# One exponential tile in 32 on VectorE: four attention layers on one Trainium2 core

## The chip, the cores and the metric

The kernel runs on one core of a Trainium2 chip. The metric is the device time of one execution in microseconds. Five engines work side by side, each through its own queue of instructions: TensorE (matmuls; PE in the profile, with its weight loads as PEld), VectorE (DVE), ScalarE (ACT), GpSimd (POOL) and SyncE (SP), which here issues the DMA transfers.

## The reference

`x` is 2048 tokens by 512. Four attention layers with a residual follow one another: windowed (A), full (B), windowed, full. Each has 32 heads of 16 dimensions. All is float32.

```python
def layer(x, wqkv, wo, window):                 # A: window 256 and causal; B: no mask
    qkv = (layernorm(x) @ wqkv).reshape(B, S, 3, H, Dh)
    q, k, v = ...
    scores = jnp.einsum("bhqd,bhkd->bhqk", q, k) * (Dh ** -0.5)
    p = softmax(scores, axis=-1)                # A: masked scores at -1e9
    return x + (p @ v -> B, S, D) @ wo
x = layer(layer(layer(layer(x, A), B), A), B)
```

## The kernel before, in words

**Attention in a full layer.** Keys lie on the partitions. A query chunk `c` (four of 512 queries) and a quad `qd` (eight of four heads) are worked through key tile by key tile: `NT` = 16 tiles `j` of 128 keys. For each tile, `exps` (L705) is called for two pairs of heads. Each call makes the scores of two heads, 128 keys by 2 x 512 queries, in PSUM (L714, two matmuls of 64 contracted rows each, which occupy the array's two row halves) and one exponential of 128x1024 on ScalarE (L718) into an SBUF tile `e`. Queries and keys are split in fp16 parts, and a shift that keeps the exponential in range stands in one of the 64 rows, so the exponential needs only its scale. Score tiles rotate over three PSUM buffers in a full layer (two of the pool `s` and `PH["third"]`), `e` tiles over six.

The values are the second matmul, `pv` in `attn_full` (L750, the matmul at L758): for each of the four heads, 17 weight columns (16 dimensions and a column of ones, which sums the denominators) against the head's half of an `e` tile, in fp32, accumulated over the 16 key tiles. Each head has its own 32 columns of the array and its own 32 partitions of one PSUM bank, `acc[0]`. The profile has two matmul records for each such fp32 matmul.

**Order on TensorE.** It is written out by hand. `attention` puts each tile's `pv` in a queue, `pvq`; `flush(2)` issues the one that is two tiles old. So the values of tile `j` come behind the scores of tile `j + 2`. Behind the last `pv` of a quad stands `epilogue` (L677): VectorE transposes `acc[0]` into SBUF (L686), divides by the denominators and writes the fp16 parts of the output `o`.

**Side work.** Between the steps, `Side.step` puts in matmuls of other stages: projections of queries, keys and values for this or the next layer, and output projections. In a full layer these run as four matmuls of 32 columns each (L429), here called a side group, all into one PSUM bank, `acc[1]`, which VectorE then empties (L527 and L528 for queries and keys, L638 for values, L652 and L673 for the output). `share` decides how many groups a step gets, from a budget and a planned clock (`clock`, `spent`), in which a step takes at least 1.8 us; `PH["free"]` keeps the bank unused for 1.6 or 2.2 us of planned time after each accumulation. `Side.one` picks the first ready piece of work. Layer 1 goes through all eight quads of one query chunk and then to the next chunk; layer 3 goes through two quads (a pair, `t`) for all four chunks and then to the next pair. Layer 1's side work includes the first projections of windowed layer 2.

**Other engines.** On the engines other than TensorE the order of instructions comes from the program order and from priorities; `tc.high_priority(HEAD_START)` moves an instruction ahead in it. In the full layers ScalarE has the exponentials alone, and VectorE the evictions, the epilogues, residual additions, statistics and normalisations.

Of the kernel before, what the change touches and what calls it, by code (L numbers as in the profile page):

```python
# [32 lines left out]
HEAD_START = 100  # L33
EB, XB, XNB, WB, VB, OB = 6, 4, 4, 2, 3, 5
L_MIN = 2.0 ** -90
L_SUM = 2.0 ** 60
# [150 lines left out]
def fast_path(ctx, tc, flag, a_x, a_wqkv, a_wo, b_wqkv, b_wo, out):  # L187
# [19 lines left out]

    XC, XN, V, O, OT, KM, PH = {}, {}, {}, {}, {}, {}, {"free": 0.0}
    CM, DN, DC, WT, ST, pend = {}, {}, {}, {}, {}, []

    clock, DONE, XNR, ONR = [0.0], {}, {}, {}
# [286 lines left out]
    def project(l, s, c, act, ht=None, first=None):  # L498
# [14 lines left out]
        for t in range(NHT) if ht is None else (ht,):  # L513
# [8 lines left out]
            e = first[2][:, t:t + 1] if first else es[:, ty, s, t:t + 1]  # L522
            with tc.high_priority(HEAD_START):
                if act:
                    nc.scalar.activation(sp[:, 0], ps, AF.Copy, scale=e)  # L525
                else:
                    nc.vector.tensor_scalar(sp[:, 0], ps, e, None, op0=ALU.mult)  # L527
                nc.vector.scalar_tensor_tensor(sp[:, 1], ps, e, sp[:, 0], op0=ALU.mult, op1=ALU.subtract)  # L528
# [28 lines left out]
    def keys(l, c, act, ht=None, first=None):  # L557
        sqs = yield from project(l, 1, c, act, ht, first)

        def rest():  # L560
            ph = squares(f"k{l}_{c}_{ht}", sqs)
            if l not in KM:
                KM[l] = vp.tile([P, NQ], F32, name=f"km{l}", tag="km", bufs=2)
            r = quarters(ht)
            with tc.high_priority(HEAD_START):
                nc.vector.tensor_reduce(KM[l][r, c:c + 1], ph[r], axis=AX.X, op=ALU.max)  # L566
        pend.append((clock[0] + 3.6, rest))
# [73 lines left out]
    def wo(l, c, tail):  # L641
# [4 lines left out]
        for i in range(4):  # L646
# [3 lines left out]
            k = 4 * c + i  # L650
            with tc.high_priority(HEAD_START):
                nc.vector.tensor_tensor(d, ps, gcol[l % 2], ALU.mult)  # L652
# [25 lines left out]
    def epilogue(l, c, qd, a):  # L678
# [5 lines left out]
        ot = vp.tile([P, QC // 32, 32], F32, name=f"ot{n}", tag="oe")  # L684
        with tc.high_priority(HEAD_START if l % 2 else 0):
            nc.vector.transpose(ot.rearrange("p b r -> p (b r)"), a)  # L686
# [19 lines left out]
    def exps(name, kt, qt, pr, pieces):  # L706

        turn["s"] += 1
        ps = PH["third"] if PH["full"] and turn["s"] % 3 == 0 else ps_s.tile([P, 2, QC], F32, name=f"s{name}", tag="s")
        w0 = min(p[3] for p in pieces)  # L710
        w1 = max(p[3] + p[2] for p in pieces)
        for kc, qc, wd_, s0 in pieces:
# [3 lines left out]
        spent(0.27)  # L716
        e = pp.tile([P, 2, QC], F32, name=f"e{name}", tag="e", bufs=EB)
        nc.scalar.activation(e[:, :, w0:w1], ps[:, :, w0:w1], AF.Exp, scale=SCALE)  # L718
# [30 lines left out]

    def attn_full(l, c, qd, kt, qt, a):  # L750
        for j in range(NT):
            es_ = []
            for pr in range(2):
                es_.append(exps(f"{l}_{c}_{qd}_{j}_{pr}", kt[j // 8], qt, pr, [(j % 8 * P, 0, QC, 0)]))

            def pv(j=j, es_=es_):
                for h in range(4):
                    nc.tensor.matmul(a[32 * h:32 * h + DH + 1, :], V[l, qd // 4, j // 8][:, j % 8, 4 * (qd % 4) + h, :],  # L758
                                     es_[h // 2][:, h % 2, :], start=(j == 0), stop=(j == NT - 1),
                                     skip_group_check=True)  # L760
            yield pv

# [4 lines left out]
    def attn_win(l, c, qd, kt, qt, a):  # L767
        first = True
        for u, tiles in enumerate(WTILES):
            tiles = [p for p in tiles if c or p[0] >= 0]  # L770
            es_ = []
            for pr in range(2):
# [4 lines left out]
                for b, far in edges:  # L777
                    v = ev[:, :, b, :]
                    with tc.high_priority(HEAD_START):
                        if far:  # L780
# [6 lines left out]

            def pv(u=u, tiles=tiles, es_=es_):
                for x, (j, q, nb, s) in enumerate(tiles):
                    for h in range(4):  # L790
# [4 lines left out]
                                         skip_group_check=True)  # L795
            yield pv

# [62 lines left out]
    class Side:  # L860

        def __init__(self, steps, works=(), following=(), least=0.0):
            self.next, self.least = list(following), least
            self.q, self.steps, self.cost, self.spent, self.k = [], steps, 0.0, 0.0, 0
            self.budget = self.lag = 0.0
            for w in carried:
                self.add(w)
# [87 lines left out]
    def attention(l, works):  # L955
# [5 lines left out]
        for t in range(NHT if l == 3 else 1):  # L961
            for c in range(NQ):
                qds = range(2 * t, 2 * t + 2) if l == 3 else range(NQD)
                if l == 1:
# [8 lines left out]
                for qd in qds:  # L973
# [149 lines left out]
    def side1():  # L1123
        a = [Q(1, c, False) for c in (2, 3)]
        for c in range(3):
            a += [OO(1, c), T(2, c), K(2, c, False), VV(2, c, False)] + ([Q(2, c, False)] if c < 2 else [])
        return a
# [67 lines left out]
```

## Time and profile before

| | |
|---|---|
| runs, median (lowest to highest of 3) | 2769.51 us (2764.41 to 2773.06) |
| profiled execution, its own time | 2767.5 us |
| its span, first to last instruction | 2765.8 us |
| mean granted TensorE clock | 0.992 |
| TensorE busy | 2629.3 us, 95% of the span |
| ScalarE busy | 2377.9 us, 86% |
| VectorE busy | 959.7 us, 35% |
| GpSimd busy | 567.7 us, 21% |
| first full layer (layer 1), exponentials | from 507 to 1458 us |
| second full layer (layer 3), exponentials | from 1792 to 2747 us |

A row of a group in the profile reads: line, engine, operation, tiles (out<-in) and shapes, xcount, then busy time and mean ns of one, then the idle time of the engine before them and what ended it. A row of the timeline reads: start, length, engine, line, operation, tiles, xcount; neighbours are merged, so the length is from the first start to the last end of the count. A row for stretches of time reads: stretch, its length, then for each engine the busy time and the number of instructions, the granted clock, the share of the DMA engines and GB/s.

### The profile page before, as it was taken

How to read it: one execution, taken by the hardware profiler on the slowest of the kernel's cores; microseconds unless marked ns; L12 is line 12 of the kernel's file. 1: busy time of each engine (PE TensorE's matmuls, PEld its weight loads, DVE VectorE, ACT ScalarE, POOL GpSimd, SP SyncE). 2: the span in 40 equal slices, each digit the busy share in tenths (PEclk: the TensorE clock that was granted, in tenths of full speed). 3: DMA queues.
4: the chain of work that ended last, by engine and by line, in shares of the span. 5: the costliest groups of instructions: out<-in, count | busy, mean ns of one | idle time of the engine just before them, and what ended most of it. 6: DMA issues, size and time to landing. Idle time of an engine off the chain costs nothing.

```text
span 2765.8 us, 59954 instructions
## 1 busy us (share of the span) xinstructions
PE 2629.3 (95%) x24502; PEld 779.9 (28%) x24502; DVE 959.7 (35%) x2063; ACT 2377.9 (86%) x2683; POOL 567.7 (21%) x1129
## 2 busy tenths in 40 slices
PE   8989989999999999999998888899999999999997
PEld 4333334322222222222223333422222222222221
DVE  7678765112131113112215676512222222222122
ACT  3666655799999999999995677399999999999997
POOL 2577662000000000000005677100000000000000
PEclk9999999999999999999999999999999999999999
DMA  7877775422232123212325564623333343333331
GB/s 225 224 244 227 224 202 161 139 70 89 85 100 88 63 81 108 85 60 91 101 68 177 149 186 133 177 66 112 105 117 116 120 124 104 102 107 114 99 96 56
DMA packets 318542, 345.32 MB, mean 125 GB/s; under 512 B 113072, under 2 KB 234416, under 8 KB 312240
## 3 DMA queue, kind: packets, MB, share of 16 engines
q1 hardware_dynamic: 318256, 341.39, 41.0%
q8 instruction: 194, 3.18, 0.5%
q14 instruction: 92, 0.75, 0.1%
HBM read 228.59 MB, written 96.99 MB: 118 GB/s over the span
## 4 chain that ended last, share of the span: by engine, by line
PE 74%; ACT 8%; issue 6%; DVE 6%; POOL 3%; DMA 3%; SPq 0%; ACTq 0%; DVEq 0%; POOLq 0%
PE acc L758 30%; PE s L714 19%; PE acc L429 10%; PE b L432 9%; ACT e L718 7%; PE acc L791 3%; PE bs L432 1%; POOL e L781 1%; POOL e L784 1%; DVE ot L686 1%; POOL wr L344 1%; DMA w<-wd 1%; DVE xh L469 1%; DVE sp L528 0%; DVE xn L463 0%
## 5 line engine op out<-in xcount | busy, mean ns | idle before, releaser
L718 ACT ACTIVATE e<-s 128x1024 f32<-128x1024 f32 (+2 forms) x2432 | 2245.6, 1115 | 106.4 <-PE s L714 98.4
L758 PE MATMUL acc<-e,vt 128*17 128x512 f32 x8192 | 1078.8, 598 | 4.9 <-DVE ot L686 4.1
L714 PE MATMUL s<-qt,kt 64*128 64x512 f16 (+3 forms) x5504 | 777.8, 355 | 68.2 <-ACT e L718 40.0
L714 PEld LDWEIGHTS <-kt 64*128 64x128 f16 x5504 | 203.1, 94 | 807.4 <-issue 776.0
L784 POOL TENSOR_SCALAR_AFFINE_SELECT e<-e 128x256 f32<-128x256 f32 x512 | 230.4, 457 | 116.0 <-ACT e L718 115.3
L758 PEld LDWEIGHTS acc<-e,vt 128*17 128x17 f32 x8192 | 136.2, 95 | 383.6 <-issue 351.8
L686 DVE STREAM_TRANSPOSE ot<-acc 128x512 f32<-128x512 f32 x128 | 91.3, 714 | 374.6 <-PE acc L758 308.5
L781 POOL TENSOR_SCALAR_AFFINE_SELECT e<-e 128x256 f32<-128x256 f32 x448 | 196.8, 445 | 91.0 <-ACT e L718 89.5
L702 POOL TENSOR_TENSOR oh<-o,oh 128x512 f16<-128x512 f32 x31 | 36.0, 1161 | 860.2 <-DVE oh L701 860.2
L791 PE MATMUL acc<-e,vt 128*17 128x384 f32 (+2 forms) x2816 | 202.0, 393 | 6.1 <-POOL e L781 4.0
L432 PE MATMUL b<-xc,w 128*128 128x512 f16 x684 | 159.4, 384 | 16.8 <-DMA w<-wd 7.8
L533 POOL TENSOR_TENSOR sq_h<-sp_h 128x512 bf16<-128x512 f16 x27 | 28.1, 1041 | 510.8 <-DVE sp_h L527 510.8
L525 ACT ACTIVATE sp<-b,es 128x512 f16<-128x512 f32 x57 | 39.2, 688 | 96.0 <-PE b L432 93.7
L527 DVE TENSOR_SCALAR sp<-acc,es 128x512 f16<-128x512 f32 x28 | 20.9, 748 | 288.9 <-PE acc L429 288.9
L638 DVE COPY vt<-acc 128x256 f32<-128x256 f32 (+1 forms) x40 | 20.2, 504 | 288.9 <-PE acc L429 288.9
L527 DVE TENSOR_SCALAR sp_h<-acc,es 128x512 f16<-128x512 f32 x27 | 20.3, 751 | 277.8 <-PE acc L429 277.1
L533 POOL TENSOR_TENSOR sq<-sp 128x512 bf16<-128x512 f16 x28 | 29.1, 1041 | 396.9 <-DVE sp L527 396.9
L429 PE MATMUL acc<-xc,w_h 128*32 128x512 f16 x1296 | 108.1, 379 | 2.3 <-DVE km L566 2.3
L429 PE MATMUL acc<-xc,w 128*32 128x512 f16 x1344 | 108.9, 379 | 0.3
L673 DVE TENSOR_TENSOR dx<-acc,gcol 128x512 f32<-128x512 f32 x60 | 41.5, 692 | 176.7 <-PE acc L429 176.7
L429 PE MATMUL acc<-wv,xc 128*32 128x256 f16 (+1 forms) x1920 | 101.7, 306 | 0.0
L429 PE MATMUL acc<-wo,oh 128*32 128x512 f16 x1296 | 101.3, 379 | 0.0
(167 smaller groups left out, 1767.0 us busy)
## 6 DMA issues: line engine op xcount, KB each, us to landing
kt<-kf SPq DMA_DIRECT2D x128, 512.0 KB
qt<-qs SPq DMA_DIRECT2D x128, 256.0 KB
xd<-x SPq DMA_DIRECT2D x96, 256.0 KB
x<-xd SPq DMA_DIRECT2D x96, 256.0 KB
w<-wd SPq DMA_DIRECT2D x20, 1024.0 KB
kt<-kw SPq DMA_DIRECT2D x64, 256.0 KB
qs<-sp SPq DMA_DIRECT2D x48, 256.0 KB
wo<-wd SPq DMA_DIRECT2D x12, 1024.0 KB
```

The lines of the kernel that those rows point to most:

```text
L429: nc.tensor.matmul(ps[g:g + 32], a[:, g:g + 32], b, start=(i == 0), stop=(i == len(pairs) - 1), skip_group_check=True)
L432: nc.tensor.matmul(ps, a, b, start=(i == 0), stop=(i == len(pairs) - 1))
L527: nc.vector.tensor_scalar(sp[:, 0], ps, e, None, op0=ALU.mult)
L533: nc.gpsimd.tensor_tensor(sq, sp[:, 0], sp[:, 0], ALU.mult)
L673: nc.vector.tensor_tensor(d, ps, gcol[1], ALU.mult)
L686: nc.vector.transpose(ot.rearrange("p b r -> p (b r)"), a)
L714: nc.tensor.matmul(ps[:, h, s0:s0 + wd_], kt[R * h:R * h + R, pr, kc:kc + P], qt[R * h:R * h + R, pr, qc:qc + wd_], start=True, stop=True)
L718: nc.scalar.activation(e[:, :, w0:w1], ps[:, :, w0:w1], AF.Exp, scale=SCALE)
L758: nc.tensor.matmul(a[32 * h:32 * h + DH + 1, :], V[l, qd // 4, j // 8][:, j % 8, 4 * (qd % 4) + h, :], es_[h // 2][:, h % 2, :], start=(j ...
L781: nc.gpsimd.affine_select(v, v, pattern=[[0, 2], [-1, P]], compare_op=ALU.is_gt, fill=0.0, base=0, channel_multiplier=1)
L784: nc.gpsimd.affine_select(v, v, pattern=[[0, 2], [1, P]], compare_op=ALU.is_ge, fill=0.0, base=0, channel_multiplier=-1)
L791: nc.tensor.matmul(a[32 * h:32 * h + DH + 1, q * P:(q + nb) * P], V[l, (4 * c + j) // 4][:, j % 4, 4 * qd + h, :], es_[h // 2][:, h % 2, s ...
```

## The change

In each quad of layer 3, and of the first three query chunks of layer 1, the exponential of the second pair of heads at key tile `JX` = 5 is computed on VectorE. `exps` is split in two: `scores` makes the matmuls, and `exps_vector` turns them into exponentials: a clamp and a scaling to base 2 that reads PSUM, then per half a rounding to an integer by a large added constant, a shift of that integer into the exponent bits, and a polynomial of degree six in the remainder, all in a single SBUF buffer `EX` taken from the tag `vw`.

The values of tile 5 are split as well: heads 0 and 1 (pair 0, from ScalarE) are done in their turn, and heads 2 and 3 (pair 1, from VectorE) are held until behind the values of tile `JX + LATE` = 14.

Around this: the head start of priorities is 300 instead of 100 in full layers (`head`); planned time for values is 0.5 us for each pair, inside the call instead of in `flush`; a piece of side work that has been chosen is kept until it yields a cost that is not positive (`within`); ahead of the last query chunk of layer 1 the value queue is emptied and `EX` given back, and one value projection of layer 2 (`VV(2, 2)`) waits for that.

```diff
+LOG2E = 1.4426950408889634
+MAGIC = 1.5 * 2 ** 23 + 127
+POLY = (...)
+JX, LATE = 5, 9
...
+    head = lambda: 3 * HEAD_START if PH["full"] else HEAD_START
...
-            with tc.high_priority(HEAD_START):
+            with tc.high_priority(head()):            # L523, L565, L651
...
-        with tc.high_priority(HEAD_START if l % 2 else 0):
+        with tc.high_priority(head() if l % 2 else 0):   # L685
...
     def exps(name, kt, qt, pr, pieces):
+        ps = scores(name, kt, qt, pr, pieces)
+        w0 = min(p[3] for p in pieces)
+        w1 = max(p[3] + p[2] for p in pieces)
+        e = pp.tile([P, 2, QC], F32, name=f"e{name}", tag="e", bufs=EB)
+        nc.scalar.activation(e[:, :, w0:w1], ps[:, :, w0:w1], AF.Exp, scale=SCALE)
+        return e
+
+    def scores(name, kt, qt, pr, pieces):
         turn["s"] += 1
         ps = PH["third"] if PH["full"] and turn["s"] % 3 == 0 else ps_s.tile([P, 2, QC], F32, name=f"s{name}", tag="s")
...
         spent(0.27)
-        e = pp.tile([P, 2, QC], F32, name=f"e{name}", tag="e", bufs=EB)
-        nc.scalar.activation(e[:, :, w0:w1], ps[:, :, w0:w1], AF.Exp, scale=SCALE)
-        return e
+        return ps
+
+    def exps_vector(ps):
+        with tc.high_priority(head()):
+            nc.vector.tensor_scalar(EX[0][:, 0], ps, -126.0 / (SCALE * LOG2E), SCALE * LOG2E, op0=ALU.max, op1=ALU.mult)
+        b, k2 = EX[0][:, 1, 0], EX[0][:, 1, 1]
+        for h in range(2):
+            a = EX[0][:, 0, h]
+            nc.vector.tensor_scalar(k2, a, MAGIC, None, op0=ALU.add)
+            nc.vector.scalar_tensor_tensor(a, k2, MAGIC, a, op0=ALU.subtract, op1=ALU.subtract)
+            nc.vector.tensor_scalar(k2.bitcast(I32), k2.bitcast(I32), 23, None, op0=ALU.logical_shift_left)
+            nc.vector.tensor_scalar(b, a, POLY[6], POLY[5], op0=ALU.mult, op1=ALU.add)
+            nc.vector.tensor_tensor(b, b, a, ALU.mult)
+            for k in range(4, 0, -1):
+                nc.vector.scalar_tensor_tensor(b, b, POLY[k], a, op0=ALU.add, op1=ALU.mult)
+            nc.vector.scalar_tensor_tensor(a, b, POLY[0], k2, op0=ALU.add, op1=ALU.mult)
+        return EX[0][:, 0]
 
     def flush(n):
         while len(pvq) > n:
-            spent(1.0)
             for f in pvq.popleft():
                 f()
...
     def attn_full(l, c, qd, kt, qt, a):
+        vector = l == 3 or c < NQ - 1
+        if vector and not EX:
+            EX.append(wp.tile([P, 2, 2, QC], F32, name=f"ex{l}", tag="vw", bufs=VB))
+        held = []
         for j in range(NT):
             es_ = []
             for pr in range(2):
-                es_.append(exps(f"{l}_{c}_{qd}_{j}_{pr}", kt[j // 8], qt, pr, [(j % 8 * P, 0, QC, 0)]))
-            def pv(j=j, es_=es_):
...
+                n = f"{l}_{c}_{qd}_{j}_{pr}"
+                piece = (kt[j // 8], qt, pr, [(j % 8 * P, 0, QC, 0)])
+                if vector and j == JX and pr:
+                    es_.append(exps_vector(scores(n, *piece)))
+                else:
+                    es_.append(exps(n, *piece))
+            def values(pairs, j=j, es_=es_):
+                spent(0.5 * len(pairs))
+                for pr in pairs:
+                    for h in (2 * pr, 2 * pr + 1):
+                        nc.tensor.matmul(a[32 * h:32 * h + DH + 1, :], V[l, qd // 4, j // 8][:, j % 8, 4 * (qd % 4) + h, :],
+                                         es_[pr][:, h % 2, :], start=(j == 0), stop=(j == NT - 1),
+                                         skip_group_check=True)
+            if vector and j == JX:
+                held.append(lambda f=values: f((1,)))
+                yield [lambda f=values: f((0,))]
+            elif vector and j == JX + LATE:
+                yield [lambda f=values: f((0, 1))] + held
+            else:
+                yield [lambda f=values: f((0, 1))]
...
     def one(self, force=False):
...
+            if self.within and self.within in self.q:
+                return self.piece(self.within)
...
     def piece(self, w):
...
             self.spent += abs(c)
+            self.within = w if PH["full"] and c > 0 else None
             return c
...
     def attention(l, works):
...
+                if (l, c) == (1, 3):
+                    flush(0)
+                    DONE["X"] = clock[0]
+                    EX.clear()
...
-                        pvq.append([f])
+                        pvq.append(f)
...
-            a += [OO(1, c), T(2, c), K(2, c, False), VV(2, c, False)] + ...
+            a += [OO(1, c), T(2, c), K(2, c, False), VV(2, c, False, after=["X"] if c == 2 else [])] + ...
```

More of the change, by code (lines that the diff above doesn't have):

```diff
@@ L206, in fast_path @@
             for ty in range(2) for s in range(4)}
-    XC, XN, V, O, OT, KM, PH = {}, {}, {}, {}, {}, {}, {"free": 0.0}
+    XC, XN, V, O, OT, KM, EX, PH = {}, {}, {}, {}, {}, {}, [], {"free": 0.0}
     CM, DN, DC, WT, ST, pend = {}, {}, {}, {}, {}, []
+    head = lambda: 3 * HEAD_START if PH["full"] else HEAD_START
     clock, DONE, XNR, ONR = [0.0], {}, {}, {}
@@ L650, in wo @@
             k = 4 * c + i
-            with tc.high_priority(HEAD_START):
+            with tc.high_priority(head()):
                 nc.vector.tensor_tensor(d, ps, gcol[l % 2], ALU.mult)
@@ L716, in exps @@
         spent(0.27)
-        e = pp.tile([P, 2, QC], F32, name=f"e{name}", tag="e", bufs=EB)
-        nc.scalar.activation(e[:, :, w0:w1], ps[:, :, w0:w1], AF.Exp, scale=SCALE)
-        return e
+        return ps
+    def exps_vector(ps):
+        with tc.high_priority(head()):
+            nc.vector.tensor_scalar(EX[0][:, 0], ps, -126.0 / (SCALE * LOG2E), SCALE * LOG2E, op0=ALU.max, op1=ALU.mult)
[11 more added lines that the diff above has]
+        return EX[0][:, 0]
     def flush(n):
         while len(pvq) > n:
-            spent(1.0)
             for f in pvq.popleft():
@@ L753, in attn_full @@
             for pr in range(2):
-                es_.append(exps(f"{l}_{c}_{qd}_{j}_{pr}", kt[j // 8], qt, pr, [(j % 8 * P, 0, QC, 0)]))
-            def pv(j=j, es_=es_):
[L757 to L761, printed above, removed]
+                n = f"{l}_{c}_{qd}_{j}_{pr}"
[18 more added lines that the diff above has]
+                yield [lambda f=values: f((0, 1))]
     WTILES = (((-2, 0, 1, 0), (1, 1, 3, 1)), ((-1, 0, 2, 0), (2, 2, 2, 2)), ((0, 0, 3, 0), (3, 3, 1, 3)))
@@ L778, in attn_win @@
                     v = ev[:, :, b, :]
-                    with tc.high_priority(HEAD_START):
+                    with tc.high_priority(head()):
                         if far:
@@ L788, in pv @@
             def pv(u=u, tiles=tiles, es_=es_):
+                spent(1.0)
                 for x, (j, q, nb, s) in enumerate(tiles):
@@ L795, in pv @@
                                          skip_group_check=True)
-            yield pv
+            yield [pv]
     class Work:
@@ L865, in __init__ @@
             self.budget = self.lag = 0.0
+            self.within = None
             for w in carried:
@@ L1125, in side1 @@
         for c in range(3):
-            a += [OO(1, c), T(2, c), K(2, c, False), VV(2, c, False)] + ([Q(2, c, False)] if c < 2 else [])
+            a += [OO(1, c), T(2, c), K(2, c, False), VV(2, c, False, after=["X"] if c == 2 else [])] + ([Q(2, c, False)] if c < 2 else [])
         return a
```

5 lines of the change are left out of this document (2 added, 3 removed).

## The prediction

> **What bounds the kernel now.** I read the page first, then the stretches of the two full layers stage by stage, then single steps in the timeline of TensorE.
>
> ```profile
> span 2765.8 us, 59954 instructions
> PE 2629.3 (95%) x24502; PEld 779.9 (28%) x24502; DVE 959.7 (35%) x2063; ACT 2377.9 (86%) x2683; POOL 567.7 (21%) x1129
> PE   8989989999999999999998888899999999999997
> ACT  3666655799999999999995677399999999999997
> PE 74%; ACT 8%; issue 6%; DVE 6%; POOL 3%; DMA 3%; SPq 0%; ACTq 0%; DVEq 0%; POOLq 0%
> L718 ACT ACTIVATE e<-s 128x1024 f32<-128x1024 f32 (+2 forms) x2432 | 2245.6, 1115 | 106.4 <-PE s L714 98.4
> L758 PE MATMUL acc<-e,vt 128*17 128x512 f32 x8192 | 1078.8, 598 | 4.9 <-DVE ot L686 4.1
> ```
>
> In the two full layers (nines in both rows) ScalarE and TensorE both look full, so neither row says which is the bound. The chain that ended last runs through TensorE for 74% and ScalarE for 8%, a first hint. The busy figures cannot settle it, because records overlap: 2432 activations of 1115 ns would be 2712 us, and the row has 2245.6. So I take the demand of each engine from its rate where it is not held up.
>
> ScalarE, at its densest:
>
> ```profile
> 2300.00:2400.00 100.00, 99.15 (x905) 24.06 (x903) 26.99 (x53) 100.00 (x110) 4.51 (x5) 1.00 0.38 116
> ```
>
> Columns: stretch, length, then busy (count) of PE, PEld, DVE, ACT, POOL, granted clock, DMA share, GB/s. 110 exponentials in 100 us: 0.909 us per tile.
>
> TensorE, in steps of one key tile (scores L714, then values L758, then perhaps side work L429):
>
> ```profile
> 2329.68 1.05 PE L758 MATMUL acc<-e,vt 128*17 128x512 f32 x8
> 2330.67 0.61 PE L714 MATMUL s<-qt,kt 64*128 64x512 f16 x4
> 2331.20 1.05 PE L758 MATMUL acc<-e,vt 128*17 128x512 f32 x8
> ...
> 901.13 1.05 PE L758 MATMUL acc<-e,vt 128*17 128x512 f32 x8
> 902.00 0.40 PE L429 MATMUL acc<-wv,xc 128*32 128x512 f16 x4
> 902.34 0.61 PE L714 MATMUL s<-qt,kt 64*128 64x512 f16 x4
> 902.87 1.05 PE L758 MATMUL acc<-e,vt 128*17 128x512 f32 x8
> 903.74 0.61 PE L429 MATMUL acc<-wv,xc 128*32 128x512 f16 x8
> 904.29 0.61 PE L714 MATMUL s<-qt,kt 64*128 64x512 f16 x4
> 904.83 1.05 PE L758 MATMUL acc<-e,vt 128*17 128x512 f32 x8
> ```
>
> From start to start of the values: 1.52 us with no side work, 1.74 with one group of four side matmuls, 1.96 with two. So a step costs TensorE 1.52 us and each side group about 0.215 more. ScalarE needs 2 x 0.909 = 1.82 us per step. With one side group TensorE has 0.08 us to spare, with two it is late.
>
> The side groups per stage are the L429 records divided by four. The stages are the four query chunks of layer 1 (c0 to c3) and the four pairs of quads of layer 3 (t0 to t3), 128 steps each:
>
> ```profile
> 507.05:743.68 236.63, 55.55 (x952) 27.17 (x952) 1.00 0.23 75
> 743.68:980.88 237.20, 54.51 (x672) 19.63 (x672) 1.00 0.28 87
> 980.88:1217.04 236.16, 54.97 (x680) 19.80 (x680) 1.00 0.29 85
> 1217.04:1457.70 240.66, 59.27 (x756) 22.16 (x760) 1.00 0.27 86
> 1792.42:2034.70 242.28, 56.62 (x912) 26.42 (x912) 0.99 0.33 99
> 2034.70:2276.40 241.70, 59.28 (x960) 27.64 (x960) 1.00 0.38 114
> 2276.40:2512.40 236.00, 47.15 (x576) 16.75 (x576) 1.00 0.37 112
> 2512.40:2746.70 234.30, 31.63 (x336) 9.76 (x336) 1.00 0.28 88
> ```
>
> Of these, 144 groups in c0 and 96 each in t0 and t1 are only 256 wide (the half-width value projections of the work lists). Their matmul is 104 ns shorter, so they count 0.11:
>
> ```profile
> L429 PE MATMUL acc<-xc,w 128*32 128x512 f16 x1344 | 108.9, 379 | 0.3
> L429 PE MATMUL acc<-wv,xc 128*32 128x256 f16 x1344 | 56.3, 275 | 0.0
> ```
>
> TensorE's demand is 194.6 us (128 x 1.52) plus side work: c0 230.6, c1 230.7, c2 231.2, c3 235.2, t0 233.6, t1 236.2, t2 225.6, t3 212.7. ScalarE's is 256 x 0.909 = 232.7 in each. The two stand within 1.5% of each other in six stages of eight. What was measured is 1.6 (t3) to 8.7 us (t0, with the layer's start) above the larger. Only t2 and t3 are plainly ScalarE's. That is the point on which the forecast rests.
>
> **The change, part by part.**
>
> *ScalarE loses one exponential in 32*, in 24 quads of layer 1 (c0 to c2) and all 32 of layer 3. Its demand in those stages falls to 248 x 0.909 = 225.4 us. That is worth at most 56 x 0.909 = 50.9 us, if nothing else stood behind it.
>
> *TensorE gets an extra pass.* The values of a key tile are now, once per quad, done as two heads (key tile 5, pair 0) and two heads nine tiles later (behind tile 14's four). What does a call with two heads cost, if one with four costs 0.87 us? A short stretch of the timeline answers it, with the full-array fp32 matmuls from the start of the kernel, as the chain merges them and as a group:
>
> ```profile
> 902.87 0.62 PE L758 MATMUL acc<-e,vt 128*17 128x512 f32 x4
> ...
> 20.73 3.43 PE b L432 x8
> L432 PE MATMUL b<-xT,wr 128*128 128x512 f32 x32 | 14.4, 592 | 0.0
> ```
>
> The first row is the answer for 902.86 to 902.90 us: four of the eight matmuls have begun within 0.04 us, one per head, and the other four are not there yet. A head has its own 32 columns of the array; the four run side by side, in two passes of some 0.43 us. One fp32 matmul over the whole array takes 3.43 / 8 = 0.43 us as well, so a pass is not shorter when fewer run beside it. Two heads therefore cost the same 0.87 us as four, and a quad has 17 such calls where it had 16. At tile 14 the held heads use the same columns as the two heads just issued, and queue behind them. That is 56 x 0.87 = 48.7 us more TensorE work, 7.0 us per stage. Bounds: half of it (0.43) if two heads streamed twice as fast, 0.98 if the call also paid the change into the scores (2330.67 less 2329.68, the call and the way to the scores). I take 0.87, by the full-array row.
>
> The Trainium skill, TensorEngine Tiling (Array Packing), section Tiling Modes, says that tiles operate independently and that different tiles can load and multiply in parallel. Taken at its word, side matmuls could use the two idle column groups; the trace agrees with it for four heads at once, and shows no call with two. By it the sum would come to 2741 us; the third rival below is this as a mechanism.
>
> *VectorE's chain.* One read of the scores, 128x1024 from PSUM, and per half three one-source operations, six with a scalar and a tensor, one product.
>
> ```profile
> L638 DVE COPY vt<-acc 128x512 f32<-128x512 f32 x11 | 7.6, 692 | 120.2 <-PE acc L429 120.2
> L638 DVE COPY vt<-acc 128x256 f32<-128x256 f32 x12 | 5.1, 422 | 82.1 <-PE acc L429 82.1
> L463 DVE TENSOR_SCALAR xn<-x,mv,y 128x512 f32<-128x512 f32 x12 | 6.6, 548 | 0.3
> L674 DVE TENSOR_TENSOR x<-x,dx 128x512 f32<-128x512 f32 x60 | 41.5, 692 | 2.0
> L528 DVE SCALAR_TENSOR_TENSOR sp_h<-acc,es,sp_h 128x512 f16<-128x512 f32 x27 | 20.3, 751 | 0.9
> 743.68:980.88 237.20, 234.51 (x2218) 53.24 (x2216) 49.47 (x115) 236.12 (x257) 10.89 (x10) 1.00 0.28 87
> ```
>
> The read is 692 + 2 x 270 = 1.23 us by the two copies. A half is 3 x 0.55 + 7 x 0.70 = 6.55, so the chain is 14.3 us; 15.0 with 0.75 for the seven. Scores of tile 5 to the held values is 11 steps (nine tiles, and the queue of two), 20.4 us at 237.2 / 128 a step. VectorE had 49.5 us of other work in the stage, 6.2 per quad, part of it the quad's epilogue in the first steps, ahead of the chain. Some 4 us of other work fall into the 20.4, so the chain ends about 2 us in time. I cost it at nothing; its cover is LATE, and without it TensorE would stand at the held values, in order. The score buffer is free again after 1.23 us against 0.909; there are three, so nothing.
>
> *Evictions behind the chain.* Side groups share one PSUM bank, and a VectorE operation of 0.70 us may stand ahead of each eviction. VectorE goes from 49.5 to 49.5 + 8 x 14.3 = 164 of 237 us in the stage. Around 150 evictions in both layers, half of them met, 0.35 us on average, give 26 us if TensorE stood still for all of it; the planner leaves 1.6 to 2.2 us ahead of the bank's next use, which is nearly the two evictions (748 + 751 ns in layer 1). Between 0 and 26 I take 2, near the lower end, by that gap.
>
> *The emptied queue ahead of c3.* The value queue is flushed once, so TensorE waits for the last exponentials and ScalarE for new scores. The end of the last layer shows such a drain:
>
> ```profile
> 2745.17 3.47 PE L758 MATMUL acc<-e,vt 128*17 128x512 f32 x24
> ```
>
> Three calls in 3.47 instead of 2.6 us: 0.9 us there, and one exponential's time until ScalarE runs again. 0 to 3, taken 2.
>
> *The rest:* the larger head start orders VectorE's evictions further ahead, the chosen piece is kept to its end, and one value projection of layer 2 waits until c3, where its input comes from c2 anyway. No transfer is added, nothing moves past SP's or GpSimd's queue. Nothing, with the evictions above as cover.
>
> **Sum.** TensorE's demand becomes c0 237.6, c1 237.7, c2 238.2, t0 240.6, t1 243.2, t2 232.6, t3 219.7, against 225.4 of ScalarE: TensorE alone is now the bound, but for t3. Above the larger I add what stages lost: 1.6 us where one engine led by 9% (t3 before), 5.5 where they were close (c3, t1). For a lead of 3 to 8% I take 2.5, for t0 with its start 4.5, and 3 in t2 and t3. Stages after less before: c0 240.1 - 236.6 = +3.5; c1 +3.0; c2 +4.5; c3 +2.0 (the drain); t0 245.1 - 242.3 = +2.8; t1 +4.0; t2 -0.4; t3 228.4 - 234.3 = -5.9. Together +13.5, with the evictions +15.5. The profiled execution took 2767.5 us (span 2765.8), 2.0 under the median of the runs: 2767.5 + 15.5 = 2783. The measurement tells about 0.3% (8 us) from no change.
>
> **Rivals.**
> 1. *The slack is used up, and no more:* the stages lose 1.6 us or less beyond the demand and evictions cost nothing. Then 2.5 falls to about 1 in c0 to c2, t0 and t1, 3 to 1.6 in t2 and t3, and the drain is free: 2783 - 2 - 7.5 - 2.8 - 2 = 2769, no change. For it: TensorE then has one clear bound. Against: c3 and t1, TensorE's already, lost 5.5.
> 2. *VectorE is late.* Where the normalisation of a query chunk falls into the 20.4 us (three quads of layer 1), four times 0.55 + 0.54 + 0.69 and the small ones, some 9 us, stand beside the chain. At 2 us spare each such quad would hold TensorE up to 7 us: +21, so 2804. It decides once other work in the interval passes 6 us. Against: the normalisation may lie behind the chain.
> 3. *The other side: the extra pass is hidden* because side matmuls fill the idle columns. TensorE's demand stays and ScalarE's falls: c0 233.1, c1 233.2, c2 233.7, t0 238.1, t1 238.7, t2 228.6, t3 228.4, c3 +2: together -28.5, with evictions 2741. It decides where the pass costs less than about 0.55 us instead of 0.87 (six stages of eight quads, 48 x 0.32 = 15.5). Against: a side group needs all four column groups, two of them still streaming.
>
> **How the numbers follow.** Forecast 0.50, rival 1 0.22, rival 2 0.15, rival 3 0.13. The forecast's own range is 2775 to 2798 (1 or 5.5 instead of 2.5 in those five stages). Over all cases 2752 leaves out most of rival 3, 2806 covers rival 2. Faster is rival 3 and a little of 1: 0.16. Same is most of 1 and the forecast's lower edge: 0.28. Slower: 0.56.
>
> **What would show it.** Right: in a quad's first step the values appear as x12 with 1.75 us to the next work; exponentials per 100 us in c1 to t1 fall to about 103 (248 in 240); score matmuls wait less for ScalarE; t3 alone is shorter. Wrong: the two-head call followed by other matmuls in clearly under 0.87 us; waits of the values for VectorE's tile (rival 2); c1 and c2 shorter than 236 us.

## The result, and the profile after

The changed kernel is slower: 2847.3 us (median of 4 runs, 2846.63 to 2850.54) against 2767.9 beside it (4 runs, 2764.41 to 2773.06). The ratio is 1.0288, with a 95% interval of 1.0269 to 1.0307, or +79 us where +15.5 was forecast.

The page of the changed kernel: the span, busy time, VectorE's slices, the chain that ended last, and three groups.

```profile
span 2844.8 us, 61013 instructions
PE 2676.1 (94%) x24502; PEld 781.6 (27%) x24502; DVE 1680.8 (59%) x3239; ACT 2345.5 (82%) x2627; POOL 573.3 (20%) x1129
DVE  7678665445665656632216667456666666656765
PE 68%; DVE 15%; ACT 6%; issue 5%; POOL 3%; DMA 3%; SPq 0%; ACTq 0%; DVEq 0%; POOLq 0%
L746 DVE SCALAR_TENSOR_TENSOR ex<-ex 128x512 f32<-128x512 f32 x448 | 310.0, 692 | 13.2
L437 PE MATMUL acc<-xc,w_h 128*32 128x512 f16 x1296 | 118.6, 381 | 14.8 <-DVE vt L646 9.4
L437 PE MATMUL acc<-wv,xc 128*32 128x256 f16 (+1 forms) x1920 | 116.4, 307 | 5.8 <-DVE vt L646 5.8
```

VectorE has 721 us more work, 12.9 per quad, and on the chain that ended last it went from 6% to 15%. The side matmuls (L437 here, L429 before) now have idle time ahead of them that ends with a VectorE eviction. Before, there was next to none.

The same eight stages as in the prediction, side matmuls alone:

```profile
507.96:758.42 250.46, 61.90 (x952) 28.61 (x952) 1.00 0.22 71
758.42:1006.45 248.03, 59.76 (x660) 20.73 (x660) 1.00 0.27 83
1006.45:1253.86 247.41, 61.55 (x684) 21.87 (x684) 1.00 0.26 83
1253.86:1491.85 237.99, 57.54 (x728) 21.16 (x729) 1.00 0.26 85
1830.85:2084.87 254.02, 62.34 (x912) 27.84 (x912) 0.99 0.30 92
2084.87:2340.91 256.04, 65.01 (x960) 29.23 (x960) 1.00 0.36 108
2340.91:2591.74 250.83, 55.70 (x576) 18.86 (x576) 0.99 0.35 107
2591.74:2825.80 234.06, 37.81 (x336) 11.42 (x336) 1.00 0.29 89
```

By stage: c0 +13.8, c1 +10.8, c2 +11.3, c3 -2.7, t0 +11.7, t1 +14.3, t2 +14.8, t3 -0.2. Layer 2, between them, is 4 us longer. The count of side matmuls is the same in layer 3 and 1% lower in layer 1 (3024 for 3060); the loss is where they are many (c0 to c2, t0 to t2), and nothing where they are few (t3) or where there is no chain (c3).

### The profile page after: what moved, and what is told of

The parts are those of the page before. It is cut to its first block, busy times and chain, and to the rows that moved or that the text cites. A ratio compares the mean times of both kernels' runs of the same rounds, so it can differ in the third digit from the quotient of the medians.

```text
span 2844.8 us, 61013 instructions
## 1 busy us (share of the span) xinstructions
PE 2676.1 (94%) x24502; PEld 781.6 (27%) x24502; DVE 1680.8 (59%) x3239; ACT 2345.5 (82%) x2627; POOL 573.3 (20%) x1129
## 4 chain that ended last, share of the span: by engine, by line
PE 68%; DVE 15%; ACT 6%; issue 5%; POOL 3%; DMA 3%; SPq 0%; ACTq 0%; DVEq 0%; POOLq 0%
PE acc L798 28%; PE s L728 17%; PE b L440 10%; PE acc L437 9%; ACT e L720 5%; PE acc L838 3%; DVE ex L746 3%; PE bs L440 2%; DVE ex L736 1%; DVE ot L694 1%; DVE ex L744 1%; DVE ex L741 1%; POOL e L827 1%; POOL e L830 1%; POOL wr L352 1%
## 5 line engine op out<-in xcount | busy, mean ns | idle before, releaser
L720 ACT ACTIVATE e<-s 128x1024 f32<-128x1024 f32 (+2 forms) x2376 | 2213.2, 1044 | 213.1 <-PE s L728 208.2
L728 PE MATMUL s<-qt,kt 64*128 64x512 f16 (+3 forms) x5504 | 768.9, 356 | 66.2 <-ACT e L720 41.0
L728 PEld LDWEIGHTS <-kt 64*128 64x128 f16 x5504 | 191.7, 94 | 787.1 <-issue 762.7
L746 DVE SCALAR_TENSOR_TENSOR ex<-ex 128x512 f32<-128x512 f32 x448 | 310.0, 692 | 13.2
L736 DVE TENSOR_SCALAR ex<-s 128x1024 f32<-128x1024 f32 x56 | 68.5, 1224 | 157.6 <-PE s L728 145.1
L541 POOL TENSOR_TENSOR sq_h<-sp_h 128x512 bf16<-128x512 f16 x27 | 31.3, 1158 | 551.6 <-DVE sp_h L535 551.6
L437 PE MATMUL acc<-xc,w_h 128*32 128x512 f16 x1296 | 118.6, 381 | 14.8 <-DVE vt L646 9.4
L437 PE MATMUL acc<-xc,w 128*32 128x512 f16 x1344 | 117.6, 379 | 9.1 <-DVE sp L536 7.6
L437 PE MATMUL acc<-wv,xc 128*32 128x256 f16 (+1 forms) x1920 | 116.4, 307 | 5.8 <-DVE vt L646 5.8
L437 PE MATMUL acc<-wo,oh 128*32 128x512 f16 x1296 | 111.8, 379 | 2.4 <-DVE m L586 1.2
L440 PEld LDWEIGHTS <-w 128*128 128x128 f16 x720 | 68.0, 99 | 114.6 <-issue 35.5
L536 DVE SCALAR_TENSOR_TENSOR sp<-b,es,sp 128x512 f16<-128x512 f32 x57 | 42.3, 746 | 93.6 <-ACT sp L533 90.1
```

The source lines that it names most:

```text
L437: nc.tensor.matmul(ps[g:g + 32], a[:, g:g + 32], b, start=(i == 0), stop=(i == len(pairs) - 1), skip_group_check=True)
L440: nc.tensor.matmul(ps, a, b, start=(i == 0), stop=(i == len(pairs) - 1))
L541: nc.gpsimd.tensor_tensor(sq, sp[:, 0], sp[:, 0], ALU.mult)
L728: nc.tensor.matmul(ps[:, h, s0:s0 + wd_], kt[R * h:R * h + R, pr, kc:kc + P], qt[R * h:R * h + R, pr, qc:qc + wd_], start=True, stop=True)
L736: nc.vector.tensor_scalar(EX[0][:, 0], ps, -126.0 / (SCALE * LOG2E), SCALE * LOG2E, op0=ALU.max, op1=ALU.mult)
L746: nc.vector.scalar_tensor_tensor(b, b, POLY[k], a, op0=ALU.add, op1=ALU.mult)
```

## The experiments

Theory P: the split of the values costs a call of TensorE per quad. Theory V: VectorE's chain stands in front of the evictions of the side bank, and TensorE, in order, stands behind them. Theory L: relief of ScalarE is worth little by itself. The rival to all of them is the planning that came with the change. Differences below are against runs of the kernel before that were taken beside each. Their intervals are some 3 to 6 us to either side.

**The split alone.**

```diff
-                    es_.append(exps_vector(scores(n, *piece)))
+                    es_.append(exps_held(scores(n, *piece)))      # ScalarE's exponential into EX
```

> The changed kernel with the second pair of tile 5 on ScalarE again (into the changed kernel's buffer EX); nothing is left on VectorE. The values stay split and held, so a quad has 17 calls. Theory P (two heads cost a whole call, and nothing in the step nets it): +0.85 us in 56 quads on the time before, 2768 + 48 = 2816 us, with the first step of a quad at 2.8 us as in the changed kernel. If TensorE's slack over the quad nets part of the pass, as the prediction summed it: about 2790. Theory V (all of the loss is VectorE's chain in front of evictions): 2768.

2804.7 us, ratio 1.0126 (1.0109 to 1.0143), +36.5 us or 0.65 per quad. It costs, but less than P's 0.85.

**The chain alone.**

```diff
-                    es_.append(exps_vector(scores(n, *piece)))
+                    ps5 = scores(n, *piece)
+                    exps_vector(ps5)
+                    e5 = pp.tile([P, 2, QC], F32, name=f"e{n}", tag="e", bufs=EB)
+                    nc.scalar.activation(e5, ps5, AF.Exp, scale=SCALE)
+                    es_.append(e5)
...
+            yield [lambda f=values: f((0, 1))]                     # always
```

> The changed kernel with ScalarE doing all exponentials and the values unsplit (16 calls); VectorE computes its chain on the same scores for nothing, the result is not used. Theory V (evictions wait behind chain operations and TensorE's side matmuls behind them): +25 to +35 us on the time before, 2793 to 2803, seen as waits between values and side matmuls. Theory P alone: 2768 to 2772.

2813.1 us, 1.0162 (1.0145 to 1.0179), +44.9. More than V expected, and as it turned out, partly for a reason of this experiment's own (below).

**The exponential left out.**

```diff
-                    es_.append(exps_vector(scores(n, *piece)))
+                    scores(n, *piece)
+                    es_.append(es_[0])
...
+            yield [lambda f=values: f((0, 1))]
```

> The changed kernel with the second pair's exponential of tile 5 left out: the values of its heads use the first pair's tile, the scores are still made; values unsplit, no chain. It is the price of one exponential in 32 by itself. Summed by stages as in the prediction (larger of the two demands): about -28 us, 2740. If relief at one step is mostly lost because three score buffers carry little of it to other steps (theory L): -8 to -18, 2750 to 2760.

2764.5 us, 0.9982 (0.9973 to 0.9992), -3.7. Less than even theory L expected. Of the stages, c1 is 237.2 us as before, t1 241.8; only t2 (232.9 for 235.4) and t3 (229.3 for 233.5, first to last score matmul) get shorter. Was the relief lost because three score buffers carry it to no other step, or was there none to have? In c1, ScalarE's idle time ahead of its exponentials rose from 1.1 us (with the planning alone, below) to 6.9, most of the 8 x 0.909 us left out, and the steps kept their length: 1.76 us with one side group and 1.95 with two in both runs, the steps behind tile 5 included. So c1 was TensorE's already, and so, by their times, were t0 and t1 and nearly c0 and c2 (each within 1 us of the planning alone). Where ScalarE was plainly the bound, in t3, 4 of 7.3 us came through.

**The planning alone.**

```diff
-                    es_.append(exps_vector(scores(n, *piece)))
+                    es_.append(exps(n, *piece))
...
+            yield [lambda f=values: f((0, 1))]
```

> The changed kernel's planning alone: head start 300, the chosen piece kept, values' planned time in the call, the queue emptied ahead of c3 and the projection that waits for it; all exponentials on ScalarE, values unsplit, no chain. Theories P, V and L: 2768 to 2772. If the planning itself costs, more than 2785.

2769.2 us, 1.0002 (0.9992 to 1.0011). The planning by itself is out.

**No extra call in layer 3.**

```diff
+                elif vector and l == 3 and j == JX:
+                    es_.append(exps_held(scores(n, *piece)))       # ScalarE, into a buffer of its own
...
-                held.append(lambda f=values: f((1,)))
-                yield [lambda f=values: f((0,))]
+                held.append(lambda f=values: f((0, 1) if l == 3 else (1,)))
+                yield [] if l == 3 else [lambda f=values: f((0,))]
```

> The changed kernel with all four heads of tile 5 held behind tile 14 in layer 3 (the first pair's exponential goes into a buffer of its own), so that a quad of layer 3 has 16 calls again; layer 1 as in the changed kernel. If the extra pass costs as work that TensorE must do (the split alone measured +36.5 us in 56 quads, 0.65 each): -21 us on the changed kernel, about 2826. If it costs as a heavy step (two calls in one step, which stays, ahead of which a step without a call cannot be saved up): 2842 to 2848.

2829.8 us, 1.0228 (1.0211 to 1.0246): +62.7 instead of +79.4, so 16.7 us came back in 32 quads, 0.52 each. The pass costs as work, although the step with two calls stays: TensorE's busy time in layer 3 fell from 958 to 939 us. Its waits ahead of side matmuls fell as well, by 12 us, but those for score buffers rose by 11.

**More planned time for the bank.**

```diff
-                PH["free"] = clock[0] + after
+                PH["free"] = clock[0] + after + 1.5                # on the chain alone
```

> The kernel with the chain alone (2813 us), and the planner keeps the side bank unused for 1.5 us more after each accumulation in the full layers. Theory V (the 45 us are mainly side matmuls that stand in TensorE's queue behind evictions which stand behind chain operations): the waits between values and side matmuls, 31 us in the two layers, fall below 10, and the time to 2790 to 2798. If side work that is put off only piles up at the ends of stages, or if the chain costs by something else (the score buffer, the clock, slower engines): 2810 or more.

2808.7 us, 1.0151 (1.0134 to 1.0168), +41.6. Missed as a whole, by layers it splits: layer 1, from its first to its last score matmul, went from 974.7 us with the chain alone to 959.4, though 112 side matmuls, some 6 us, were put off into layer 2; layer 3 went from 972.7 to 977.5. There each pair of quads and query chunk must finish its side work before the next, so put-off work probably piled up; that was not followed.

**The chain's read alone.**

```diff
-        b, k2 = EX[0][:, 1, 0], EX[0][:, 1, 1]
-        for h in range(2):
-            ...                                                     # the twenty operations
```

> The kernel with the chain alone, but only the chain's first operation, the read of the score buffer by VectorE; the twenty operations behind it are left out. If the score buffer that is given back late costs by itself (waits for score buffers rose by some 13 us with the chain): 2778 to 2785. If it is only the twenty operations in front of the evictions and of this read: 2768 to 2773.

2788.3 us, 1.0077 (1.006 to 1.0094), +21.2. ScalarE's waits in this run show most of it:

```profile
ACT e L782 <- DVE ex L736: 15.4, 33, 1.5
```

ScalarE's exponential waited 15.4 us in total for VectorE's read of the same score tile. The changed kernel has one reader for each tile, so this is no part of its cost. It makes the chain alone too dear, and the next three runs were built on the kernel without the exponential instead.

**The smaller head start.**

```diff
-    head = lambda: 3 * HEAD_START if PH["full"] else HEAD_START
+    head = lambda: HEAD_START if PH["full"] else HEAD_START
```

> The kernel with the chain alone, with the head start of priorities at 100 as before instead of 300. Theory V: evictions are ordered later among the chain's operations, so slower than 2813, 2820 to 2850. If the order among VectorE's operations does not matter: 2813.

2817.5 us, 1.0184 (1.0167 to 1.0201), +50.4 against +44.9. The 5 us are less than V expected, and within the noise of the two.

**Relief with the chain, with its read alone, with the split.**

```diff
-                    es_.append(exps_vector(scores(n, *piece)))
+                    exps_vector(scores(n, *piece))                  # chain, or its read alone
+                    es_.append(es_[0])
```

```diff
+                    scores(n, *piece)                               # split, no chain
+                    es_.append(es_[0])
...
+                yield [lambda f=values: f((0, 1)), lambda f=held[0], e=es_: f((1,), es_=e)]
```

> The changed kernel without the split: the chain runs on VectorE in the exponential's place, but its result is not used; the values of its heads use the first pair's tile, in one call. In the kernels with the chain alone ScalarE's exponential of that tile waited for VectorE's read (15 us in the read alone), which the changed kernel does not have; here it is gone. If the chain's cost in the changed kernel is the remainder, 79.4 - 36.5 + 3.7 = 47 us: 2764.5 + 47 = 2811. If the 45 us of the chain alone came half from that wait: 2785 to 2795, and the rest of the remainder belongs to chain and split together.

> As the kernel with relief and chain, with only the chain's first operation, VectorE's read of the scores. If VectorE's read gives the score buffer back too late: 2775 to 2785. If the 21 us of the read alone came from ScalarE waiting behind it: 2764 to 2768.

> The changed kernel without the chain: the second pair's exponential of tile 5 left out, the values split and held as in the changed kernel, the held heads on tile 14's second pair. If relief and split add up (-3.7 and +36.5): 2801. If the idle ScalarE lets TensorE absorb part of the pass: 2780 to 2790; if the split takes even the 3.7 us of the relief: 2805.

Chain: 2797.2 us, 1.0111 (1.0095 to 1.0126), +30.8. Read: 2763.1, 0.9986 (0.9976 to 0.9995), -3.3, as without it: the score buffer is given back in time. Split: 2799.7, 1.0114 (1.0098 to 1.0129), +33.3. With the relief at -3.7, the chain costs 30.8 + 3.7 = 34.5 us, nearly all of it the twenty operations behind the read, and the split 37.0. With relief they add up to 67.8; the changed kernel has 79.4, so 11.6 belong to chain and split together. That is a remainder of four measurements, good to some 8 us.

The next two views are the full layers with relief, without the chain and with it (PE, PEld, DVE, ACT, POOL):

```profile
508.00:1457.00 949.00, 937.97 (x9190) 222.75 (x9188) 183.56 (x425) 927.53 (x1000) 47.50 (x46) 1.00 0.27 83
1796.00:2742.00 946.00, 931.72 (x8939) 227.28 (x8937) 222.16 (x439) 918.53 (x991) 45.47 (x42) 1.00 0.34 104
```

```profile
503.90:1472.00 968.10, 942.47 (x9193) 222.77 (x9196) 495.03 (x929) 929.39 (x1001) 50.66 (x47) 1.00 0.26 82
1811.00:2774.00 963.00, 936.83 (x8931) 226.32 (x8931) 631.25 (x1111) 920.68 (x990) 48.92 (x42) 1.00 0.34 102
```

19 us in layer 1 and 17 in layer 3, with the same instructions on TensorE and ScalarE. The wait is at one place: from a values call to the side matmuls behind it. Summed over the two layers (time beyond the usual 0.87 us from a values call's start, where it is over 0.06), it is 7 us without the chain, 40 with it, 45 in the changed kernel and 1 with relief and split. The first difference, 33 us, is nearly the 34.5 of the chain. The second, 44 us, is nearly what the chain adds to relief and split: 34.5 and the 11.6 of their meeting.

What ended TensorE's waits in the changed kernel, the two largest groups ahead of side matmuls:

```profile
PE acc L437 <- DVE vt L646: 15.2, 12, 1.7
PE acc L558 <- POOL sq_h L541: 9.3, 9, 1.2
```

The first is the bank that has not been emptied; with VectorE's other evictions this kind makes 31 us. The second goes one engine further: GpSimd squares what VectorE has evicted, and a side matmul sums the squares. With relief and split no wait of this kind is left in layer 3; there the eviction starts 0.10 us behind its matmuls on average and the square takes 1.04 us, in the changed kernel 0.77 and 1.16. So most of this delay, too, is the late eviction. With relief and chain, 10.6 us are of this kind (3.6 without the chain), and one wait of 4.2 us in layer 1 ended with a DMA, which was not followed.

**The bank's planned time in layer 1, half the chain, a larger head start, narrow operations.** All four on relief with the chain.

```diff
+                PH["free"] = clock[0] + after + (1.5 if PH["l"] == 1 else 0)
...
+        for h in range(1):                                          # half the chain
...
+    head = lambda: 30 * HEAD_START if PH["full"] else HEAD_START
...
+        for h, g in ((0, 0), (0, 1), (1, 0), (1, 1)):               # narrow: 256 columns
+            w = slice(g * QC // 2, (g + 1) * QC // 2)
+            a, b, k2 = EX[0][:, 0, h, w], EX[0][:, 1, 0, w], EX[0][:, 1, 1, w]
```

> The kernel with relief and chain (2797 us), with the side bank kept unused for 1.5 us more after each accumulation, in layer 1 only. Theory V (the chain's 34 us are side matmuls waiting in TensorE's order for evictions that stand behind chain operations; the trace shows 18 us of such waits in layer 1): layer 1 gets back most of its 19 us, 2780 to 2785. If the waits are not the cause but go along with it: 2795 to 2800.

> The kernel with relief and chain, with the chain for the first half only: the read and ten operations instead of twenty. Theory V: an eviction meets the chain half as often, so half of the 34 us or less: 2773 to 2782. If the cost comes when VectorE's whole load or the end of the chain passes some point, not from each operation: 2764 to 2769.

> The kernel with relief and chain, with a head start of 3000 instead of 300 in the full layers. If evictions are ordered behind several chain operations because their priority is too low: 2770 to 2785. If the order comes from when the planner thinks that they are ready, with priority only among the ready: 2795 to 2800.

> The kernel with relief and chain, with the chain's twenty operations cut to 256 columns each: forty, some 0.42 us each instead of 0.69. If an eviction waits only for the operation in progress: its wait falls by 40%, 2780 to 2786. If several operations are ordered ahead of it: the chain is longer in total, 2795 to 2812.

The gap: 2788.8 us, 1.0073 (1.0052 to 1.0095), 8.4 us less than without it. The total is a little outside V's bounds; by layers:

```profile
509.00:1459.00 950.00, 935.10 (x9077) 222.40 (x9076) 492.76 (x927) 926.25 (x1000) 50.46 (x47) 1.00 0.27 83
1806.00:2769.00 963.00, 936.72 (x8931) 226.09 (x8927) 631.53 (x1111) 920.92 (x990) 48.98 (x42) 1.00 0.34 102
```

Layer 1 is back at the time it has without the chain (950 for 968, VectorE's work unchanged), while layer 3, without the gap, stayed. The waits behind values calls fell from 19 us to 3 in layer 1 and stayed at 21 in layer 3. But not all of the 18 us is waits: 112 side matmuls (9077 for 9193 on TensorE), some 6 us, were put off into layer 2, which became 7 us longer. Layers 1 and 2 together gained 10 us. So the waits are a cause and not only a companion, and the gap gets back about half of what they cost in layer 1.

Half the chain: 2770.8, 1.0011 (1.0001 to 1.0021), +3.8, so 7.5 us above relief; half the operations cost a fifth, not a half, and the time lies between the two expectations. The waits behind values calls are 17 us here, 10 more than with relief alone. Head start 3000: 2799.4, 1.0116 (1.0099 to 1.0133): a larger head start does not bring the evictions forward. Narrow: 3021.2, 1.092 (1.0899 to 1.094), far above either expectation, with 200 us of waits behind values calls. Not all of its loss is waits: its granted clock was 0.97 in layer 1 and 0.94 in layer 3, where the chain with relief had 1.00, and TensorE was busy 59 us longer in the two; why was not tried. One eviction of that kernel, on VectorE and on TensorE:

```profile
2024.35 0.42 DVE L741 SCALAR_TENSOR_TENSOR ex<-ex 128x256 f32<-128x256 f32 x1
...
2027.37 1.43 DVE L746 SCALAR_TENSOR_TENSOR ex<-ex 128x256 f32<-128x256 f32 x4
2028.71 0.42 DVE L747 SCALAR_TENSOR_TENSOR ex<-ex 128x256 f32<-128x256 f32 x1
2029.05 0.42 DVE L746 SCALAR_TENSOR_TENSOR ex<-ex 128x256 f32<-128x256 f32 x1
2029.38 0.42 DVE L646 COPY vt<-acc 128x256 f32<-128x256 f32 x1
```

```profile
2024.18 1.05 PE L799 MATMUL acc<-e,vt 128*17 128x512 f32 x8
2029.86 1.47 PE L437 MATMUL acc<-xc,w_h 128*32 128x512 f16 x12 [4.62 <-DVE vt L646]
```

The copy that empties the bank stands behind a row of chain operations, and TensorE behind the copy for 4.6 us. VectorE's order is fixed before the kernel runs. Counting the chain operations that start between the end of a bank's last matmul and its eviction in layer 3: with half the chain 29 of 103 evictions have any ahead, at most 3; with the chain 62, up to 4; in the changed kernel 57, up to 4; with narrow operations 34, up to 37. So the evictions that meet the chain do not become more in the narrow kernel, but each can have far more of it in front. That would fit a VectorE that is late against what the order was made for, because the planner takes these operations for shorter than they are; this was not tried.

**Only where TensorE has slack.**

```diff
-        vector = l == 3 or c < NQ - 1
+        vector = l == 3 and qd >= 6                                 # and no extra call, as above
```

> The exponential on VectorE only where TensorE has slack, the last two quads of layer 3 (eight quads), with all four heads of tile 5 held, so that no call is added. The exponential left out gained some 5 us in that stage (t3); the chain's cost there is small, since evictions are few: 2763 to 2767. If the chain costs there what it costs on average (0.8 us a quad): 2768 to 2772.

2768.4 us, 1.0003 (0.9994 to 1.0012): no difference. The relief of one tile in every quad was worth 3.7 us without any cost beside it, so no arrangement of this change could gain much more than that.

## Why the prediction was wrong

The direction was right (slower, the extra pass as a cost), the size was not: 15.5 against 79.4. Two terms of the sum failed, the relief and the evictions. The prediction's own stages without the extra pass come to -28.5 us (its rival 3, the drain ahead of c3 included), so the pass stands in its sum with 13.5 + 28.5 = 42.0 and the evictions with 2. Measured were -3.7, 37.0, and 34.5 + 11.6 = 46.1. Of the 63.9 us that are missing, 24.8 are relief that did not come and 44.1 are evictions; the pass gave 5.0 back. By its steps, in the order of its sum:

- **What bounds the kernel, and the relief: this step failed in its size.** It had the two engines close in six stages, then TensorE alone. But the sum then let what the stages lose above the larger demand fall from 3.5 to 8.7 us to 2.5 (4.5 in t0), as if ScalarE's closeness were the reason. With the relief alone c1 and t1 did not move at all, and ScalarE only stood longer. There the excess is TensorE's own; of what it consists is open.
- **The extra pass: mechanism right, 37.0 us instead of 48.7 of work, of which 42.0 stood in the sum.** Part of it is hidden, as rival 3 had it, by side matmuls in the idle columns. How much is not separated: with the split the waits behind values calls also fell, from 7 us to 1. A two-head call of the changed kernel:

```profile
2162.61 0.61 PE L798 MATMUL acc<-e,vt 128*17 128x512 f32 x2
2162.63 0.40 PE L437 MATMUL acc<-wv,xc 128*32 128x256 f16 x4
2163.05 0.60 PE L798 MATMUL acc<-e,vt 128*17 128x512 f32 x2
2163.06 0.91 PE L437 MATMUL acc<-wv,xc 128*32 128x256 f16 x8
```

  Side matmuls start 0.02 us behind the two heads. The Trainium skill, TensorEngine Tiling (Array Packing), Tiling Modes, says so: tiles operate independently. The trace agrees. But a side group needs all four column groups (of the first four side matmuls behind the heads' second pass, two start at 2163.06 and two only at 2163.48), and 0.65 of the 0.87 us per quad stays. Side matmuls this soon are a sign that the prediction had named for being wrong. It had also netted the pass against ScalarE's demand in t3; over all stages the pass measured the same with the relief in place (37.0) as without (36.5).
- **The chain in time: right.** It came out at 12.9 us per quad (14.3 forecast), and the values waited for it next to never. The waiters of the tile `ex`:

```profile
POOL vt L629: 54.5, 1
DVE m L586: 13.0, 6
DVE km L574: 2.4, 1
PEld acc L798: 0.3, 1
```

  Only the last is values that wait for the chain. The first is a memset on GpSimd that waits for the buffer to be given back; GpSimd has 3% of the chain that ended last, as before. In the other two VectorE waits for TensorE, at evictions of sums of squares, where the profile names a values call that reads `ex` as what ended the wait.
- **The score buffer, the flush, the planning: right at about nothing.** VectorE's read -3.3 beside -3.7, the planning, with the emptied queue in it, +1.
- **Evictions behind the chain: this step failed, and is the larger miss.** The prediction had one operation of 0.70 us ahead of an eviction, 0.35 on average, bounded the whole at 26 us and took 2, because the planner's gap covers one. In the changed kernel it is up to four. What follows on TensorE and on VectorE behind the two-head call above:

```profile
2164.45 1.05 PE L798 MATMUL acc<-e,vt 128*17 128x512 f32 x8
2166.73 0.61 PE L437 MATMUL acc<-xc,w_h 128*32 128x512 f16 x8 [1.23 <-DVE vt L646]
```

```profile
2162.74 2.87 DVE L746 SCALAR_TENSOR_TENSOR ex<-ex 128x512 f32<-128x512 f32 x4
2165.65 0.69 DVE L747 SCALAR_TENSOR_TENSOR ex<-ex 128x512 f32<-128x512 f32 x1
2166.26 0.42 DVE L646 COPY vt<-acc 128x256 f32<-128x256 f32 x1
```

  The bank's last side matmul ended at 2163.97 (2163.06 + 0.91), four chain operations were still to end, and the copy began at 2166.26. TensorE stood until 2166.73. By the experiments the chain cost 34.5 us by itself and 11.6 more with the split. The waits show both (33 and 44 us); why the split adds to them is not shown. Rival 2 (VectorE late) looked at the wrong waiter: not the held values, but the bank.

Relief -3.7, split 37.0, chain 34.5, both together 11.6: 79.4 us. The last is by its making what is left over.

## What to carry to other kernels

Before moving work to an engine that looks idle, ask what that engine does for the bound engine and how soon it must: 35% busy says nothing of the wait when an eviction gets behind a chain whose order was fixed beforehand. Price such a wait by the longest run of operations that can stand ahead of it, not by half of one. And measure the relief by itself first, by leaving the work out: here that run would have ended the idea at 3.7 us.

## What the runs showed of the hardware that was not expected

- Side matmuls start 0.02 us behind a two-head call, while it runs (shown above), as the column groups that it leaves idle would allow.
- One-source fp32 operations on 512 columns with constants took 0.42 us, where the prediction went by 0.55 of a form with scalars read per partition. A cut to 256 columns took an operation of two sources only from 692 to 422 ns, so some 150 ns of each are fixed. The Trainium skill, VectorE: DVE Perf Modes, The perf-mode tier table, has fp32 one-source operations in SBUF at twice the rate of those with two sources. The first two rows, both of the changed kernel, agree with it once the 150 ns are taken off: some 275 and 540 ns. The third row is of the narrow operations.

```profile
L740 DVE TENSOR_SCALAR ex<-ex x112: 416/427/605, 518.1 to 2813.8; 128x512 f32<-128x512 f32 x112
L744 DVE TENSOR_TENSOR ex<-ex x112: 680/692/695, 520.1 to 2815.8; 128x512 f32<-128x512 f32 x112
L746 DVE SCALAR_TENSOR_TENSOR ex<-ex 128x256 f32<-128x256 f32 x896 | 344.9, 422 | 1.6
```

- GpSimd's squares of layer 3 took 1158 ns in the changed kernel instead of 1041 before, and 1168 with the chain and relief. Why was not tried.

```profile
L541 POOL TENSOR_TENSOR sq_h<-sp_h 128x512 bf16<-128x512 f16 x27 | 31.3, 1158 | 551.6 <-DVE sp_h L535 551.6
```
